# Second-layer weight sums as a stream of short steps, and another order of products in the last chunk

## The chip, the cores and the metric

The kernel runs on one core of one Trainium2 chip. Time is device time of one execution in microseconds, taken as the median of several runs of the same program. A core has five engines that run side by side, each through its own list of instructions in order: TensorE (PE; its weight loads are shown as PEld), VectorE (DVE), ScalarE (ACT), GpSimd (POOL) and SyncE (SP), which issues most DMAs here. Engines wait for one another and for DMAs by semaphores. An instruction that waits holds up all that stand behind it on its engine.

## The reference

```python
def _moe_ref(x, domain_probs, w1, w2):
    p = domain_probs / (domain_probs.sum(-1, keepdims=True) + 1e-09)
    for e in range(E):
        h = np.maximum(x @ w1[e], 0.0)
        out += p[:, e:e + 1] * (h @ w2[e])

def reference(**kwargs):
    attn_out = _attn_ref(**attn_kwargs)          # block-sparse attention
    x = attn_out.transpose(0, 2, 1, 3).reshape(B * S, H * D)
    return _moe_ref(x=x, **moe_kwargs)
```

The attention has 4 batches, 8 heads, 768 positions and 64 columns a head, with blocks of 32 positions of which each sees its neighbours, the first, the last and three sampled ones. Then 3072 tokens of 512 columns go through 4 experts of two layers, 512 to 1024 to 512, weighted by `p` and summed.

## The kernel before

**Stages.** Attention of batch 0 comes first. From then on the experts of batch b run on TensorE with the attention of batch b + 1 mixed in. The hidden columns of the four experts are cut into `NCH` = 8 chunks of 512 columns, so that a batch of experts is 8 chunks of a first layer and a second layer.

**Two-part numbers.** TensorE gets each 32-bit operand as a rounded part (a cast on ACT, L507, L543, L604, L750) and the remainder (a subtraction on POOL or DVE, L508, L544, L605, L751). Three products of parts stand for one.

**Seven products for eight.** The first layer, but for chunk 0, takes 7 products of sums of blocks where a plain 2 by 2 block product takes 8 (Strassen and Winograd). The second layer of batch 0 is plain: `second` multiplies the hidden values `hh`, `hl` by the weights `w2o` into `po`, and DVE adds the result into `oacc` (L674, L676). The second layer of batches 1 to 3 takes seven products a chunk and half (`second7`); it needs sums of blocks of `w2`.

**Where the sums are made.** During batch 0 each weight tile is split once and written back to DRAM, to be loaded ready-made for later batches: `keep1` for the first layer, `keep2` for the second (`kept2`). `split_w2` makes the plain tiles (`w2o`), and `sums_w2(c, j)` makes the sums of a pair of tiles: four subtractions `r` on DVE (L564 to L567), then for each of two tiles of 512 columns a cast `t` on ACT (L543), a subtraction on POOL (L544) and a write of 512 KB (L548). `second` calls it at two moments of every chunk, after the last product of the first and of the second tile of the half `g` = 1; after the second one the four tiles `r2` of the next chunk are loaded (L479). The tiles `t` have two buffers.

**What sets the order.** The order of the instructions on each engine is that in which the program makes them. For batch 0 the generator `experts` mixes steps of `first` and `second`: 114 steps of the first layer (p) and 192 of the second (q), by the rule at L838. Each step's follow-up work (emptying the bank, split, sums, loads) is put on the other engines' lists right there. PSUM has one bank each for `v` and `w` in batch 0; a first-layer product that starts afresh in `w` needs the last reader of that bank to be done.

**Later batches.** After the first layer of a chunk, `hidden` makes the seven operands `ho` of the second layer from the four blocks `ha` (a11, a21, a12, a22): sums on DVE or POOL, then cast and remainder. `STEPS` says how many first-layer products before or after the chunk's end each is made; at most `NHO` = 4 are ahead. `SEQ` is the order of the second layer's 14 products (number, half): numbers 1, 6, 7, 4 build up in one PSUM bank per half (`u`), the others in `v`, which has two banks. `TO` says into which of the four output blocks `tot` DVE adds each product (L812), `LAST` after which one a block is complete and goes out (L814). Weights `w2o` come through four buffers (L536). At the end of the last chunk no first layer is left to fill TensorE's waits.

Of the kernel before, what the change touches and what calls it, by code (L numbers as in the profile page):

```python
# [17 lines left out]
P = 128  # L18
# [5 lines left out]
def attention_moe_kernel(ctx: ExitStack, tc, qb, kb, vr, sampled, sampled_t, probs, w1, w2, out):  # L24
# [437 lines left out]
    ORDER2 = (1, 2, 5, 6, 3, 7, 4)  # L462
# [13 lines left out]
    def load_w2(n):  # L476
        if n < NCH * FT:
            r2[n] = raw.tile([P, DM], F32, name="r2", bufs=FT)
            nc.sync.dma_start(r2[n], w2[n // FT, n % FT])  # L479
# [47 lines left out]
    def again2():  # L527
        half = DM // 2
        for b in range(1, B):
            for c in range(NCH):  # L530
                for n in ORDER2:
# [14 lines left out]
    def keep2(c, which, s, j, o):  # L546
        kept2[c, which, s, j] = dram.tile([P, 2, DM], F32, name=f"kept2_{c}_{which}_{s}_{j}")
        nc.sync.dma_start(kept2[c, which, s, j], f32(o))  # L548

    def split_w2(n):  # L550
        if n >= NCH * FT:
            next(weights2)
            return
        c, f = divmod(n, FT)
        o = wp.tile([P, 2, DM], F32R, name="w2o")
        split(r2[n], o)
        w2t[c, f] = o
        keep2(c, 0, f // 2, f % 2, o)

    def sums_w2(c, j):  # L560
        half = DM // 2
        a, b = (r2.pop(c * FT + 2 * s + j) for s in range(2))
        b11, b12, b21, b22 = (r[:, d * half:(d + 1) * half] for r in (a, b) for d in range(2))
        nc.vector.tensor_sub(b11, b12, b11)  # L564
        nc.vector.tensor_sub(b12, b22, b12)
        nc.vector.tensor_sub(b22, b22, b11)
        nc.vector.tensor_sub(b21, b21, b22)  # L567
# [80 lines left out]
    def second(b, c, g, f, j):  # L648
# [95 lines left out]
    def hidden(b, c):  # L744

        end = b == B - 1 and c == NCH - 1

# [11 lines left out]
        yield  # L759
        a12, a22 = blk.pop((c, 0, 1)), blk.pop((c, 1, 1))  # L760
# [4 lines left out]
        two(5, a21, nc.vector if end else nc.gpsimd)  # L765
# [5 lines left out]
        two(3, a12, nc.vector if end else nc.gpsimd)  # L771
# [3 lines left out]
        two(4, a22, nc.vector if end else nc.gpsimd)  # L775
# [8 lines left out]
    LAST = {2: (0, 0), 3: (0, 1), 7: (1, 1), 4: (1, 0)}  # L784
# [3 lines left out]
    def second7(b, c, i):  # L788
        n, d = SEQ[i]
        w, h = w2o[b, c, n], ho[b, c, n]  # L790
        chain = n in (1, 6, 7, 4)
        if not chain:
            ps = later["m"].tile([P, HS], F32, name="v", bufs=2)
        elif n == 1:
            ps = W2[d] = later["m"].tile([P, HS], F32, name=f"u{d}", bufs=1)
        else:
            ps = W2[d]
        fresh = not chain or n == 1
# [6 lines left out]
        for g, dh in TO[n]:  # L805
            if c == 0 and d == 0 and n in FRESH:
                tot[g, dh] = later["a"].tile([P, 2, HS], F32, name="tot", bufs=4)
            t = tot[g, dh][:, d]
            if c == 0 and n in FRESH:
                nc.scalar.copy(t, ps)  # L810
            else:
                nc.vector.tensor_add(t, ps, t)  # L812
            if c == NCH - 1 and LAST.get(n) == (g, dh) and d:
                nc.sync.dma_start(bass.AP(out.tensor, out.offset + b * S * DM + dh * (DM // 2) * S + g * HS,  # L814
                                          [[S, P], [P * S, 2], [1, HS]]), tot.pop((g, dh)))
# [10 lines left out]
    def experts():  # L826
# [8 lines left out]
        while q < len(two):  # L835

            wait = after_first and p < len(one) and one[p][2] == 4 and q < ready(p - MORE)
            if wait or p >= min(len(one), (q * NCH * L + (OFF + MORE) * len(two)) / len(two)):  # L838
# [3 lines left out]
                if p == len(one) and q % 2:  # L842
                    convert(b + 1)
                yield T2, 2
            else:
# [4 lines left out]
                after_first = True  # L850
                if p == len(one):
                    only_raw.close()
# [30 lines left out]
        todo = [(e + at, n, i) for i, e in enumerate(ends) for at, n in STEPS]  # L883
# [43 lines left out]
    def spread_weights():  # L927
# [4 lines left out]
        later["t"] = batch0.enter_context(tc.tile_pool(name="tp", bufs=2))  # L932
        rows = later["t"].tile([P, P], F32, name="prows", bufs=1)
# [17 lines left out]
    with ExitStack() as only:  # L951
# [13 lines left out]
        for n in range(N + 3):  # L965
# [23 lines left out]
            if n == N - 7:  # L989
                for s in range(2):  # L990
                    load_w1(0, s)
                for f in range(FT):
# [117 lines left out]
```

## Time and profile before

| what | value |
|---|---|
| median of 3 runs | 1301.5 us (1298.95 to 1302.43) |
| the profiled execution | 1307.93 us |
| its span, first to last instruction | 1306.2 us |
| mean granted TensorE clock | 0.977 |
| HBM read / written | 258.00 MB / 67.68 MB |
| DMA, over the span | 249 GB/s |

An engine's share of busy time is a mean over stages with different limits, so the table of stages in the prediction is the thing to start from. A row of the timeline gives the start, the length, the engine and line, the operation with output and inputs, and in brackets the idle time of the engine before it with what ended it. "issue" there means that the profile shows nothing that was waited for.

### The profile page before, as it was taken

To read this page: it belongs to the slowest core of one execution; us is meant where nothing else is said; L and a number is where in the kernel's file an instruction comes from. 1 tells how busy PE (TensorE), PEld (TensorE's weight loads), DVE (VectorE), ACT (ScalarE), POOL (GpSimd) and SP (SyncE) were. 2 spreads that over 40 slices of the span, in tenths; PEclk is the share of its full clock that TensorE was granted. 3 is DMA by queue.
4 is the path that set the end of the run, shared out by engine and by line. 5 is a ranking of instruction groups with operands and counts; after the bars stand their busy time and mean duration, and the time that the engine had idled before them with its cause. 6 is when DMAs were issued, how large, how long until landed. Compare 5 with 4: busy or idle time off the path is not lost.

```text
span 1306.2 us, 32799 instructions
## 1 busy us (share of the span) xinstructions
PE 1233.0 (94%) x12575; PEld 1127.0 (86%) x12575; DVE 858.0 (66%) x1829; ACT 530.6 (41%) x1261; POOL 789.4 (60%) x703
## 2 busy tenths in 40 slices
PE   6778998998999899999999999999999999999997
PEld 3557777877887688999999989999999999999997
DVE  5456576666656556777766766767776776666665
ACT  4563545554554324444443324544443323222221
POOL 5443647565654346576764775767664777666663
PEclk9789899999999899999999999999999999999999
DMA  8666677888875877799886966989887778887774
GB/s 248 179 204 245 242 266 266 290 292 290 284 271 209 312 226 234 238 282 267 272 252 208 340 206 218 279 264 278 272 265 211 242 219 268 259 264 249 247 235 145
DMA packets 211176, 327.85 MB, mean 251 GB/s; under 512 B 18155, under 2 KB 118092, under 8 KB 211020
## 3 DMA queue, kind: packets, MB, share of 16 engines
q1 hardware_dynamic: 203936, 302.68, 72.1%
q0 software_dynamic: 7040, 23.07, 5.9%
q8 instruction: 100, 1.64, 0.5%
q14 instruction: 56, 0.46, 0.1%
q10 hardware_dynamic: 44, 0.00, 0.0%
HBM read 258.00 MB, written 67.68 MB: 249 GB/s over the span
## 4 chain that ended last, share of the span: by engine, by line
PE 79%; DVE 8%; issue 4%; DMA 3%; ACT 3%; POOL 2%; SPq 0%; DVEq 0%; ACTq 0%; POOLq 0%
PE w L586 19%; PE u L802 14%; PE v L586 14%; PE v L802 11%; PE po L656 6%; PE o L293 3%; PE tp L280 3%; PE s L258 2%; PE s L253 2%; PE sw L327 2%; DMA kept<-t 1%; PE ow L358 1%; DVE hl L605 1%; PE tw L348 1%; ACT hh L604 1%
## 5 line engine op out<-in xcount | busy, mean ns | idle before, releaser
L751 POOL TENSOR_TENSOR ho<-ha,ho 128x768 fp32r<-128x768 f32 x165 | 322.4, 1964 | 235.3 <-ACT ho L750 234.8
L586 PE MATMUL w<-xo,wo 128*128 128x384 f32 x1536 | 318.7, 344 | 24.9 <-DVE hl L605 19.0
L586 PEld LDWEIGHTS w<-xo,wo 128*128 128x128 f32 x1536 | 273.1, 190 | 38.3 <-DVE hl L605 22.4
L750 ACT CAST ho<-ha 128x768 fp32r<-128x768 f32 x168 | 139.3, 836 | 271.4 <-DVE ha L703 97.1
L586 PE MATMUL v<-xo,wo 128*128 128x384 f32 x1200 | 245.4, 341 | 2.3 <-DVE hl L605 2.1
L802 PE MATMUL u<-ho,w2o 128*128 128x384 f32 x1152 | 237.3, 341 | 3.7 <-issue 2.7
L586 PEld LDWEIGHTS v<-xo,wo 128*128 128x128 f32 x1200 | 214.3, 189 | 8.3 <-DVE hl L605 2.7
L802 PEld LDWEIGHTS u<-ho,w2o 128*128 128x128 f32 x1152 | 204.6, 188 | 6.5 <-issue 4.7
L802 PE MATMUL v<-ho,w2o 128*128 128x384 f32 x864 | 178.3, 342 | 0.0
L802 PEld LDWEIGHTS v<-ho,w2o 128*128 128x128 f32 x864 | 153.6, 189 | 1.3 <-DVE tot L812 0.3
L812 DVE TENSOR_TENSOR tot<-u,tot 128x384 f32<-128x384 f32 x180 | 99.3, 552 | 60.2 <-PE u L802 58.0
L656 PE MATMUL po<-w2o,hh 128*128 128x512 f32 x384 | 128.6, 417 | 6.5 <-DVE oacc L676 6.5
L812 DVE TENSOR_TENSOR tot<-v,tot 128x384 f32<-128x384 f32 x180 | 95.6, 550 | 58.3 <-PE v L802 56.0
L271 ACT ACTIVATE p<-p,mx 128x256 f32<-128x256 f32 (+1 forms) x192 | 95.4, 498 | 82.2 <-DVE mx L268 82.2
L703 DVE SCALAR_TENSOR_TENSOR ha<-ha,pb 128x384 f32<-128x384 f32 x126 | 122.7, 974 | 4.4
L138 POOL DMA_INDIRECT v<-in_vr_dram,vidx x88 | 85.6, 973 | 65.8 <-PE o L293 21.7
L508 POOL TENSOR_TENSOR wo<-r,wo 128x256 fp32r<-128x256 f32 x92 | 73.8, 808 | 71.5 <-ACT wo L507 67.0
L268 DVE CUSTOM_DVE_ANT_1 p<-s,mask 128x256 f32<-128x256 f32 (+1 forms) x192 | 69.7, 418 | 38.6 <-PE s L258 37.5
L656 PEld LDWEIGHTS po<-w2o,hh 128*128 128x128 f32 x384 | 71.3, 195 | 16.8 <-DVE oacc L676 8.1
L656 PE MATMUL po<-w2o,hl 128*128 128x512 f32 x192 | 77.7, 405 | 0.0
L293 PE MATMUL o<-v,pt 128*32 128x64 f32 x2816 | 56.6, 227 | 5.6 <-issue 3.4
L293 PEld LDWEIGHTS o<-v,pt 128*32 128x32 f32 x2816 | 47.8, 114 | 16.3 <-issue 12.1
(146 smaller groups left out, 1617.2 us busy)
## 6 DMA issues: line engine op xcount, KB each, us to landing
w2o<-kept SPq DMA_DIRECT2D x336, 256.0 KB
wo<-kept SPq DMA_DIRECT2D x318, 256.0 KB
kept<-wo SPq DMA_DIRECT2D x106, 256.0 KB
v<-in_vr_dram SPq DMA_DIRECT2D x44, 384.0 KB
kept<-w2o SPq DMA_DIRECT2D x32, 512.0 KB
kept<-t SPq DMA_DIRECT2D x32, 512.0 KB
r<-in_w_dram SPq DMA_DIRECT2D x16, 512.0 KB
r<-in_w_dram SPq DMA_DIRECT2D x32, 256.0 KB
```

Of the source, the lines that this page charges most:

```text
L138: nc.gpsimd.indirect_dma_start(out=v[:, i, 1], out_offset=None, in_=vr, element_offset=b * S * DM, in_offset=bass.IndirectOffsetOnAxis(ap= ...
L268: nc.vector.tensor_tensor_reduce(p.rearrange("p (a b) -> p a b", b=BLOCK), s[h][:n, i], mk, -SCALE, 3.0e38, ALU.add, ALU.min, mx[:n])
L271: nc.scalar.activation(p, p, AF.Exp, bias=mx[:n], scale=-1.0, accum_out=self.sums[:n, m:m + 1])
L293: nc.tensor.matmul(o[cs, m], self.pt[:, 2 * m + k, cs], vs[c][:, k, e], start=k == 0, stop=k == 1)
L508: nc.gpsimd.tensor_sub(o[:, 1], src, f32(o[:, 0]))
L586: nc.tensor.matmul(ps, w[:, wi, t], x[:, xi, t], start=fresh and m == 0, stop=m == 3 * KH - 1, skip_group_check=not fresh)
L656: nc.tensor.matmul(p, a[:, js], w[:, i], start=f == 0 and n == 0, stop=f == FT - 1 and n == 2)
L703: nc.vector.scalar_tensor_tensor(block(g, half), src, 0.0, q, op0=ALU.max, op1=ALU.mult)
L750: nc.scalar.copy(o[:, 0], src)
L751: eng.tensor_sub(o[:, 1], src, f32(o[:, 0]))
L802: nc.tensor.matmul(ps, w[:, j, wi, ds], h[:, hi, j], start=fresh and m == 0, stop=m == 5, skip_group_check=not fresh)
L812: nc.vector.tensor_add(t, ps, t)
```

## The change

`sums_w2` is now a generator, `spare`. It no longer uses the tiles `r2` that `split_w2` works on, but loads each pair of tiles of `w2` a second time (`r3`, 512 KB, one buffer, 16 loads). Each call of `next(spare)` does one short step: a load, five empty steps, two subtractions on DVE, two more, and then four times a cast and subtraction of 256 columns in one step and its write (256 KB, in pieces of 1 KB) in the next. That is 16 steps for a pair. `experts` calls it after each of its own steps once p is over 16 and makes what is left when the first layer of batch 0 ends. The tiles `t` become half as wide with four buffers. `r2` has three buffers, each loaded again at the end of `split_w2`.

In the last chunk of the last batch the second layer takes its products in the order `SEQ_END`: 1, 7, 4, 2, 5, 6, 3. Product 7 goes into a `v` bank and 4 is added onto it there; product 6 is the last in `u` and is added to three output blocks. So 20 additions to `tot` stand where 16 did. `hidden` makes the operands in the order 1, 7, 4, 2, 5, 6, 3, by `STEPS_END`, with one more sum on DVE.

```diff
-    ORDER2 = (1, 2, 5, 6, 3, 7, 4)
+    SEQ_END = [(1, 0), (7, 0), (1, 1), (7, 1), (4, 0), (4, 1), (2, 0), (2, 1),
+               (5, 0), (5, 1), (6, 0), (6, 1), (3, 0), (3, 1)]
+    def last_one(b, c):
+        return b == B - 1 and c == NCH - 1
...
-            r2[n] = raw.tile([P, DM], F32, name="r2", bufs=FT)
+            r2[n] = raw.tile([P, DM], F32, name="r2", bufs=3)
...
-        split(r2[n], o)
+        split(r2.pop(n), o)
         w2t[c, f] = o
         keep2(c, 0, f // 2, f % 2, o)
-
-    def sums_w2(c, j):
+        load_w2(n + 3)
+
+    def sums_w2():
         half = DM // 2
-        a, b = (r2.pop(c * FT + 2 * s + j) for s in range(2))
...
-        for s, r in enumerate((a, b)):
-            o = later["t"].tile([P, 2, DM], F32R, name="t2")
-            split(r, o)
-            keep2(c, 1, s, j, o)
+        for c in range(NCH):
+            for j in range(2):
+                r = raw.tile([P, 2, DM], F32, name="r3", bufs=1)
+                nc.sync.dma_start(r, w2[c, j::2].rearrange("s p e -> p s e"))
+                for _ in range(6):
+                    yield
+                b11, b12, b21, b22 = (r[:, s, d * half:(d + 1) * half] for s in range(2) for d in range(2))
+                nc.vector.tensor_sub(b11, b12, b11)
+                nc.vector.tensor_sub(b12, b22, b12)
+                yield
+                nc.vector.tensor_sub(b22, b22, b11)
+                nc.vector.tensor_sub(b21, b21, b22)
+                yield
+                for s in range(2):
+                    for d in range(2):
+                        cols = slice(d * half, (d + 1) * half)
+                        o = later["t"].tile([P, 2, half], F32R, name="t2", bufs=4)
+                        split(r[:, s, cols], o)
+                        yield
+                        keep2(c, 1, s, j, o, cols)
+                        yield
...
-            elif f < 2:
-                sums_w2(c, f)
-                if f == 1:
-                    for i in range(FT):
-                        load_w2((c + 1) * FT + i)
...
+        if last_one(b, c):
+            two(7, s3)
+            yield
+            a12, a22 = blk.pop((c, 0, 1)), blk.pop((c, 1, 1))
+            two(4, a22)
+            nc.vector.tensor_add(a21, a21, a22)
+            yield
+            two(2, a12, nc.vector)
+            nc.gpsimd.tensor_sub(a11, a21, a11)
+            yield
+            two(5, a21, nc.vector)
+            yield
+            two(6, a11)
+            nc.vector.tensor_sub(a12, a12, a11)
+            yield
+            two(3, a12, nc.vector)
...
+    STEPS_END = [(-5, 0), (-4, 1), (-3, 7), (0, 4), (0, 2), (0, 5), (0, 6), (0, 3)]
+    TO_END = {**TO, 6: [(0, 1), (1, 1), (1, 0)]}
+    LAST_END = {(0, 0): 2, (0, 1): 3, (1, 1): 6, (1, 0): 6}
...
+                if p > L + 2:
+                    next(spare, None)
```

How this stands on the engines is shown at three places. The first is DVE's list in chunk 0 of batch 0, at the first sums; `r` are raw weights and their sums, `mx` is attention's row maximum, `hl` and `p` belong to the first layer. Before:

```order
L503 TENSOR_TENSOR r_2249<-r_2249 128x256
L564 TENSOR_TENSOR r_1641<-r_1641 128x256
L565 TENSOR_TENSOR r_1641<-r_1645,r_1641 128x256
L566 TENSOR_TENSOR r_1645<-r_1645,r_1641 128x256
L567 TENSOR_TENSOR r_1645<-r_1645 128x256
L334 TENSOR_REDUCE mx_2714<-sw 128x1 x2
L336 TENSOR_TENSOR mx<-mx_2714 128x1
L337 TENSOR_SCALAR mx<-mx 128x1
L564 TENSOR_TENSOR r_1643<-r_1643 128x256
L565 TENSOR_TENSOR r_1643<-r_1647,r_1643 128x256
L566 TENSOR_TENSOR r_1647<-r_1647,r_1643 128x256
L567 TENSOR_TENSOR r_1647<-r_1647 128x256
```

The changed kernel's list, some steps further on, where its first sums stand (L578 to L582):

```order
L505 TENSOR_TENSOR r_2588<-r_2588 128x256
L578 TENSOR_TENSOR r_2761<-r_2761 128x256
L579 TENSOR_TENSOR r_2761<-r_2761 128x256
L691 TENSOR_SCALAR oacc<-po,pr 128x512
L581 TENSOR_TENSOR r_2761<-r_2761 128x256
L582 TENSOR_TENSOR r_2761<-r_2761 128x256
L659 TENSOR_TENSOR u_2846<-w,z_2814 128x384
```

Eight sums stood within twelve rows; now two and two stand between the layer's own instructions, and the second pair of tiles comes 16 steps later.

The second place is SP's list of DMAs around the same sums: `kept<-t` writes sums, `kept<-wo` first-layer weights, `r<-in_w` loads weights. Before:

```order
L548 DMA kept_0_1_0_0_2684<-t_2681 128x1024
L548 DMA kept_0_1_1_0_2689<-t_2686 128x1024
L548 DMA kept_0_1_0_1_2734<-t_2731 128x1024
L548 DMA kept_0_1_1_1_2739<-t_2736 128x1024
L479 DMA r_2741<-in_w_dram 128x512
L479 DMA r_2743<-in_w_dram 128x512
L479 DMA r_2745<-in_w_dram 128x512
L479 DMA r_2747<-in_w_dram 128x512
```

In the changed kernel, from the first load of a pair (`128x2x512`) to the next one's neighbourhood:

```order
L574 DMA r_2761<-in_w_dram 128x2x512
L492 DMA kept_1_1_2_2784<-wo 128x512
L492 DMA kept_1_1_1_2822<-wo 128x512
L492 DMA kept_1_1_5_2852<-wo 128x512
L555 DMA kept_0_1_0_0_2854<-t_2837 256x1x256
L492 DMA kept_1_1_6_2879<-wo 128x512
L555 DMA kept_0_1_0_0_2854<-t_2860 256x1x256
L132 DMA v<-in_vr_dram 96x2x512
L135 DMA v<-in_vr_dram 32x2x512
L555 DMA kept_1_0_0_0_2964<-w2o 128x1024
L485 DMA r_2966<-in_w_dram 128x512
L555 DMA kept_0_1_1_0_2974<-t_2968 256x1x256
```

The group of four writes and four loads is spread out: half writes alternate with other DMAs, and each plain tile's load follows the write of another.

The third place is DVE's list at the end of the program, from the last first-layer result (`ha<-w,pb`) on; the `u` and `v` are banks of second-layer products, `ho` an operand of them. Before:

```order
L703 SCALAR_TENSOR_TENSOR ha<-w,pb 128x384
L761 TENSOR_TENSOR ha<-ha 128x768
L751 TENSOR_TENSOR ho<-ha,ho 128x768
L812 TENSOR_TENSOR tot<-u_16989,tot 128x384
L812 TENSOR_TENSOR tot<-u_17025,tot 128x384
L812 TENSOR_TENSOR tot<-u_17252,tot 128x384
L812 TENSOR_TENSOR tot<-v,tot 128x384
L812 TENSOR_TENSOR tot<-u_17268,tot 128x384
L751 TENSOR_TENSOR ho<-ha,ho 128x768
```

Now:

```order
L720 SCALAR_TENSOR_TENSOR ha<-w,pb 128x384
L780 TENSOR_TENSOR ha<-ha 128x768
L852 TENSOR_TENSOR tot<-u_17149,tot 128x384
L852 TENSOR_TENSOR tot<-u_17185,tot 128x384
L766 TENSOR_TENSOR ho<-ha,ho 128x768
L852 TENSOR_TENSOR tot<-u_17411,tot 128x384
L852 TENSOR_TENSOR tot<-v,tot 128x384
L852 TENSOR_TENSOR tot<-u_17427,tot 128x384
L766 TENSOR_TENSOR ho<-ha,ho 128x768
```

The two additions that empty the `u` banks of the chunk before the last now stand ahead of the first subtraction for an operand. In both lists the bank names with the higher numbers belong to the last chunk.

More of the change, by code (lines that the diff above doesn't have):

```diff
@@ L530, in again2 @@
             for c in range(NCH):
-                for n in ORDER2:
+                for n in [n for n, d in (SEQ_END if last_one(b, c) else SEQ) if d]:
                     o = wp.tile([P, 2, 2, half], F32R, name="w2o")
@@ L544, in split, with keep2 @@
         nc.gpsimd.tensor_sub(o[:, 1], src, f32(o[:, 0]))
-    def keep2(c, which, s, j, o):
-        kept2[c, which, s, j] = dram.tile([P, 2, DM], F32, name=f"kept2_{c}_{which}_{s}_{j}")
-        nc.sync.dma_start(kept2[c, which, s, j], f32(o))
+    def keep2(c, which, s, j, o, cols=slice(0, DM)):
+        if (c, which, s, j) not in kept2:
+            kept2[c, which, s, j] = dram.tile([P, 2, DM], F32, name=f"kept2_{c}_{which}_{s}_{j}")
+        nc.sync.dma_start(kept2[c, which, s, j][:, :, cols], f32(o))
     def split_w2(n):
@@ L555, in split_w2 @@
         o = wp.tile([P, 2, DM], F32R, name="w2o")
-        split(r2[n], o)
+        split(r2.pop(n), o)
         w2t[c, f] = o
         keep2(c, 0, f // 2, f % 2, o)
-    def sums_w2(c, j):
+        load_w2(n + 3)
+    def sums_w2():
         half = DM // 2
-        a, b = (r2.pop(c * FT + 2 * s + j) for s in range(2))
[L563 to L567, printed above, removed]
-        for s, r in enumerate((a, b)):
-            o = later["t"].tile([P, 2, DM], F32R, name="t2")
-            split(r, o)
-            keep2(c, 1, s, j, o)
+        for c in range(NCH):
[19 more added lines that the diff above has]
+                        yield
+    spare = sums_w2()
     accs = {}
@@ L744, in hidden @@
     def hidden(b, c):
-        end = b == B - 1 and c == NCH - 1
         def two(n, src, eng=nc.gpsimd):
@@ L759, in hidden @@
         yield
+        if last_one(b, c):
[14 more added lines that the diff above has]
+            two(3, a12, nc.vector)
+            yield
+            return
         a12, a22 = blk.pop((c, 0, 1)), blk.pop((c, 1, 1))
@@ L764, in hidden @@
         yield
-        two(5, a21, nc.vector if end else nc.gpsimd)
+        two(5, a21)
         yield
@@ L770, in hidden @@
         yield
-        two(3, a12, nc.vector if end else nc.gpsimd)
+        two(3, a12)
         yield
@@ L774, in hidden @@
         yield
-        two(4, a22, nc.vector if end else nc.gpsimd)
+        two(4, a22)
         yield
@@ L783, in attention_moe_kernel @@
     FRESH = {1: (0, 0), 5: None, 4: (1, 0)}
-    LAST = {2: (0, 0), 3: (0, 1), 7: (1, 1), 4: (1, 0)}
+    LAST = {(0, 0): 2, (0, 1): 3, (1, 1): 7, (1, 0): 4}
+    TO_END = {**TO, 6: [(0, 1), (1, 1), (1, 0)]}
+    LAST_END = {(0, 0): 2, (0, 1): 3, (1, 1): 6, (1, 0): 6}
     W2 = {}
@@ L788, in second7 @@
     def second7(b, c, i):
-        n, d = SEQ[i]
+        last = last_one(b, c)
+        n, d = (SEQ_END if last else SEQ)[i]
         w, h = w2o[b, c, n], ho[b, c, n]
-        chain = n in (1, 6, 7, 4)
-        if not chain:
+        fresh = n not in ((6, 4) if last else (6, 7, 4))
+        if last and n in (7, 4):
+            if n == 7:
+                W2[7, d] = later["m"].tile([P, HS], F32, name="v", bufs=2)
+            ps = W2[7, d]
+        elif n not in (1, 6, 7, 4):
             ps = later["m"].tile([P, HS], F32, name="v", bufs=2)
-        elif n == 1:
-            ps = W2[d] = later["m"].tile([P, HS], F32, name=f"u{d}", bufs=1)
-        else:
+        else:
+            if n == 1:
+                W2[d] = later["m"].tile([P, HS], F32, name=f"u{d}", bufs=1)
             ps = W2[d]
-        fresh = not chain or n == 1
         m = 0
@@ L804, in second7 @@
             m += 1
-        for g, dh in TO[n]:
+        for g, dh in (TO_END if last else TO)[n]:
             if c == 0 and d == 0 and n in FRESH:
@@ L812, in second7 @@
                 nc.vector.tensor_add(t, ps, t)
-            if c == NCH - 1 and LAST.get(n) == (g, dh) and d:
+            if c == NCH - 1 and (LAST_END if last else LAST)[g, dh] == n and d:
                 nc.sync.dma_start(bass.AP(out.tensor, out.offset + b * S * DM + dh * (DM // 2) * S + g * HS,
@@ L850, in experts @@
                 after_first = True
+                if p > L + 2:
+                    next(spare, None)
                 if p == len(one):
+                    for _ in spare:
+                        pass
                     only_raw.close()
@@ L882, in experts @@
         made = used = 0
-        todo = [(e + at, n, i) for i, e in enumerate(ends) for at, n in STEPS]
+        todo = [(e + at, n, i) for i, e in enumerate(ends)
+                for at, n in (STEPS_END if i == len(ends) - 1 else STEPS)]
         gens = {}
@@ L931, in spread_weights @@
         nc.tensor.transpose(t[:n], pr.rearrange("p t e -> p (t e)"), ident)
-        later["t"] = batch0.enter_context(tc.tile_pool(name="tp", bufs=2))
-        rows = later["t"].tile([P, P], F32, name="prows", bufs=1)
+        later["t"] = batch0.enter_context(tc.tile_pool(name="tp", bufs=4))
+        rows = later["t"].tile([P, P], F32, name="prows", tag="t2", bufs=4)
         nc.scalar.copy(rows[:n], t[:n])
@@ L991, in attention_moe_kernel @@
                     load_w1(0, s)
-                for f in range(FT):
+                for f in range(3):
                     load_w2(f)
```

## The prediction

> **What bounds the kernel now.** I read the share of busy time first, then the program cut into its four stages, then TensorE's waits in the second stage, then the instructions around those waits. The table has the stretch, its length, busy time of PE, PEld, DVE, ACT and POOL with instruction counts, granted clock, DMA share and GB/s.
>
> ```profile
> span 1306.2 us, 32799 instructions
> PE 1233.0 (94%) x12575; PEld 1127.0 (86%) x12575; DVE 858.0 (66%) x1829; ACT 530.6 (41%) x1261; POOL 789.4 (60%) x703
> ...
> 117.00:461.00 344.00, 316.27 (x3023) 268.14 (x3024) 212.08 (x473) 167.11 (x428) 193.43 (x228) 0.96 0.77 268
> 461.00:1281.00 820.00, 814.92 (x7605) 781.34 (x7603) 568.76 (x1114) 297.22 (x638) 532.67 (x372) 1.00 0.81 250
> 1281.00:1306.30 25.30, 17.47 (x85) 16.14 (x84) 12.86 (x21) 3.67 (x5) 9.47 (x5) 0.89 0.45 151
> ```
>
> TensorE is the bound. From 461 to 1281 us (batches 1 to 3) it idles for 5 us of 820 at full clock, and the change leaves that stretch's order alone. What can be won lies in batch 0 (117 to 461), where it idles for 28 us and the clock is 0.96, and in the last 25 us. Its waits in batch 0 (sum, times, longest) are these, and they are nearly all of its idle time: 27.5 us.
>
> ```profile
> PE w L586 <- DVE hl L605: 17.7, 7, 3.5
> PE po L656 <- DVE oacc L676: 6.5, 2, 6.1
> PE w L586 <- DVE z L642: 3.3, 4, 1.5
> ```
>
> TensorE waits for DVE to empty a PSUM bank. The rows around the longest `hl` wait, in order of time, show what held DVE and ACT up (start, length, instruction, idle before it):
>
> ```profile
> 213.87 1.22 PE L586 MATMUL w<-xo,wo 128*128 128x384 f32 x6
> 214.63 0.42 DVE L564 TENSOR_TENSOR r<-r 128x256 f32<-128x256 f32 x1
> 216.25 1.29 POOL L544 TENSOR_TENSOR t<-r,t 128x512 fp32r<-128x512 f32 x1
> 216.43 1.40 DVE L567 TENSOR_TENSOR r<-r 128x256 f32<-128x256 f32 x1
> ...
> 224.88 0.62 ACT L543 CAST t<-r 128x512 fp32r<-128x512 f32 x1 [0.37 <-DVE r L567]
> 225.40 0.48 ACT L604 ACTIVATE hh<-w 128x384 fp32r<-128x384 f32 x1
> 225.92 0.56 DVE L605 SCALAR_TENSOR_TENSOR hl<-w,hh 128x384 fp32r<-128x384 f32 x1 [1.12 <-ACT hh L604]
> 226.53 2.29 PE L586 MATMUL w<-xo,wo 128*128 128x384 f32 x6 [3.47 <-DVE hl L605]
> ```
>
> The sums `r` (L564 to L567) and their casts `t` (L543) stand ahead of `hh` and `hl` on in-order engines. DVE's L567 takes 1.40 us beside POOL's L544. The six matmuls after the wait take 2.29 us where six before it took 1.22: the clock has dropped. The last chunk shows a second form, where the cast waits for a `t` buffer whose write to DRAM is under way:
>
> ```profile
> 439.67 1.27 SPq L548 DMA_DIRECT2D kept<-t  x2
> 446.77 0.62 ACT L543 CAST t<-r 128x512 fp32r<-128x512 f32 x1 [7.50 <-DMA kept<-t]
> 450.32 1.22 PE L656 MATMUL po<-w2o,hh 128*128 128x512 f32 x2 [6.08 <-DVE oacc L676]
> ```
>
> How much the cold clock adds is read from 8 us that begin at each restart; four of the six are
>
> ```profile
> 138.00:146.00 8.00, 8.00 (x30) 7.09 (x31) 4.60 (x8) 2.97 (x8) 3.23 (x5) 0.64 1.01 343
> 227.00:235.00 8.00, 8.00 (x32) 7.13 (x32) 3.57 (x7) 2.78 (x6) 2.93 (x5) 0.65 0.92 283
> 361.00:369.00 8.00, 7.54 (x147) 6.17 (x148) 4.09 (x14) 3.89 (x14) 5.35 (x8) 0.79 0.96 316
> 450.00:458.00 8.00, 7.64 (x24) 5.66 (x25) 7.06 (x8) 2.77 (x4) 4.02 (x2) 0.72 0.78 254
> ```
>
> These miss (1 − clock) × 8 = 2.9, 2.8, 1.7 and 2.2 us. The other two restarts (317 and 407) I take like the one at 361, 1.6 us each. Together 12.8 us. With the idle time, the sums cost batch 0 up to 27.5 + 12.8 = **40.3 us**, 2.5 us for each of the 16 pairs of sums.
>
> **The change part by part: batch 0.** These rows give count, then shortest, median and longest duration in ns:
>
> ```profile
> L507 ACT CAST wo<-r x87: 388/406/417, 100.2 to 423.6; 128x256 fp32r<-128x256 f32 x87
> L508 POOL TENSOR_TENSOR wo<-r,wo x87: 718/742/1444, 100.7 to 424.3; 128x256 fp32r<-128x256 f32 x87
> L543 ACT CAST t<-r x32: 614/619/624, 128.4 to 448.0; 128x512 fp32r<-128x512 f32 x32
> L544 POOL TENSOR_TENSOR t<-r,t x32: 1263/1286/1397, 129.1 to 448.7; 128x512 fp32r<-128x512 f32 x32
> L567 DVE TENSOR_TENSOR r<-r x16: 424/426/1397, 129.2 to 442.4; 128x256 f32<-128x256 f32 x16
> ```
>
> DVE's 64 sums stay, two to a step instead of four (or eight over two steps) in a row: 0.85 us ahead of an `hl` instead of 1.7. The 32 casts and subtractions of 512 columns become 64 of 256 columns. By the `wo` rows of that shape ACT does 64 × 0.406 = 26.0 us instead of 32 × 0.619 = 19.8, POOL 64 × 0.742 = 47.5 instead of 41.2. Both are spare: ACT is busy for 167 and POOL for 193 of 344 us. What counts is the longest piece in front of `hh` or `hl`: a cast of 0.41 instead of up to four of 0.62, and a POOL instruction of 0.74 beside which DVE may be held, instead of 1.29. The wait for `t` buffers goes, since each of the four half buffers is refilled a whole pair of sums, 16 steps, later. The stream has 16 × 16 = 256 steps, and the program offers 265 before the first layer of batch 0 ends, so nothing is left to be made in a lump there.
>
> What is late next: short steps beside attention's own work on DVE, and the new load `r3`. Nothing in the trace prices that directly. The bounds are nothing (the steps fit into slack) and all of today's 2.5 us a pair. I take the row nearest to it, the waits for `z`, where PE waited for one DVE instruction delayed by sums: 3.3 / 4 = 0.8 us. At one for each pair that leaves 16 × 0.8 = 13 us, without a colder clock. Gain: 40.3 − 13 = **27 us** (0 to 40).
>
> Two moved pieces I cost at nothing. `r2` has three buffers and is refilled behind each `keep2`; that load waits for the same POOL subtraction as the write in front of it on SP, and has three splits' time. The 64 smaller writes replace 32 on SP, where two of them took 1.27 us at 439.67; if SP ran late, the loads of `r1` and `r2` behind them would be late and ACT would stand.
>
> The new 16 loads of 512 KB and the writes of 1 KB pieces cost transfer time. Batch 0 keeps the DMA engines busy for 0.77 × 344 = 265 us. 8.4 MB at 268 / 0.77 = 348 GB/s adds 24 us. For the 16.8 MB of `t` I take 461 to 1281's 250 / 0.81 = 309 GB/s (its loads are mostly of short pieces), which adds 6 us. 295 us in a batch 0 of 317 us is a share of 0.93: it fits, but transfers will queue longer.
>
> **The last chunk.** In order of time:
>
> ```profile
> 1278.89 2.28 PE L802 MATMUL u<-ho,w2o 128*128 128x384 f32 x12
> 1279.56 0.95 DVE L761 TENSOR_TENSOR ha<-ha 128x768 f32<-128x768 f32 x1
> 1281.46 1.82 DVE L751 TENSOR_TENSOR ho<-ha,ho 128x768 fp32r<-128x768 f32 x1 [0.95 <-ACT ho L750]
> 1283.21 1.01 DVE L812 TENSOR_TENSOR tot<-u,tot 128x384 f32<-128x384 f32 x2
> 1283.85 2.23 PE L802 MATMUL u<-ho,w2o 128*128 128x384 f32 x6 [2.68 <-issue]
> 1287.58 1.22 PE L802 MATMUL u<-ho,w2o 128*128 128x384 f32 x6
> ...
> 1298.83 3.33 PE L802 MATMUL u<-ho,w2o 128*128 128x384 f32 x18
> ...
> 1302.21 0.56 DVE L812 TENSOR_TENSOR tot<-u,tot 128x384 f32<-128x384 f32 x1 [0.49 <-PE u L802]
> ```
>
> PE is free at 1281.2, but the next `u` bank is emptied by the adds at 1283.21, which stand behind L751 on DVE. The trace calls the wait "issue"; it ends when the first add does. In the new order the adds follow the 0.95 us sum directly: 1279.56 + 0.95 + 0.55 = 1281.1, in time. That removes 2.7 us, and the cold start behind it: two products from 1283.85 to 1287.58, 3.7 us, against 2 × 1.05 (the step from 12 to 18 matmuls, 3.33 − 2.28). That is 1.6 more. Operands 1 and 7 are both ready, so four products run (4.2 us). Then 4 accumulates on the bank of 7 and must wait for the add that reads it. Following DVE's new order with 0.55 for an add, 0.95 for a subtraction, I get waits of 0.8, 0.5 and 0.2 us at products 4, 2 and 5, against 2.0 us lost between 1287.58 and 1302.16 now: 0.5 won. At the end product 6 brings six adds (3.0 us) against 2.1 us of PE, so the last add ends some 0.8 us later behind PE than now. Sum: 2.7 + 1.6 + 0.5 − 0.8 = **4 us** (0 to 5.5).
>
> **Two rules of the Trainium skill weighed.** The clock: 1.81 us of idle stand ahead of the restart at 361, whose clock was 0.79.
>
> ```profile
> 361.46 1.60 PE L586 MATMUL w<-xo,wo 128*128 128x384 f32 x6 [1.81 <-DVE hl L605]
> ```
>
> The Trainium skill, "TensorE: Matmul & The Clock Gate", Part 1, says that the clock halves after about 3.4 us of idle window. By it only the waits of 3.47 and 6.08 us would cool (2.8 + 2.2 = 5.0 us instead of 12.8), and the gain would be 7.8 us smaller; the row of 361 speaks against it, and I keep 12.8. The second speaks against the change: "SBUF — State Buffer" says that DVE with two SBUF inputs and GpSimd exclude one another for a whole instruction. L567's 1.40 us beside L544's 1.29 agrees. By it POOL's 6.3 us more could all fall on DVE and take the gain from 31 to 25.
>
> **The rivals.** (a) *The second load is late.* DVE stands in order behind `r3`, loaded six steps earlier. Some 310 us for 265 steps make 1.2 us a step now and 1.07 after: 6.4 us. The worst transfer seen is the `kept<-t` above, 439.67 to 446.77, 7.1 us under full DMA. Late by about 2 us in half of the pairs (shorter steps, queues of 0.93 share): 8 × 2.2 = 18 us back, gain 31 − 18 = 13, time 1288. For it: the share; against: six steps are usually enough. (b) *Slower.* Same place, every pair: if TensorE loses more than (40.3 + 4) / 16 = 2.8 us a pair, the change loses. A load of 9 us holds DVE for 2.6 us, and TensorE then also restarts cold (12.8 / 6 = 2.1): 4.7 × 16 = 75, less 44, some 30 us slower: 1332; in three pairs of four 1313. It decides from about 8 us a load, above the worst seen. (c) *Not what it says:* attention's bursts, not sums, hold `hl`; then all 2.5 us a pair stay and 4 us of the tail count: 1298. Against: the waits stand only beside `r` and `t`.
>
> **How the numbers follow.** The profiled execution took 1307.9 us (span 1306.2), the median of the runs is 1301.5, 6.4 less. 1307.9 − 27 − 4 = 1276.9 there, **1270** as a median. Forecast (1256 to 1283) 0.62; (a) 0.20; (c) and mixtures within 0.3% 0.07; (b) 0.11. The range takes in no residue at all with the whole tail (40.3 + 5.5: 1256) and (a) with 4 us to spare: 1256 to 1292. 0.3% is about what a measurement of this kernel can tell from no change. Faster 0.82, same 0.07, slower 0.11.
>
> **What would show it.** Right: in 117 to 440 the waits of PE for `hl` fall from 17.7 to below 10 us, no cast waits for `kept<-t`, the clock there is near 1.00, batch 0 ends 25 us earlier, and no 2.68 us stand ahead of the last chunk. Wrong: waits of DVE's `r` for `r<-in_w`, ending in `hl`; a DMA share near 1; POOL's subtractions as the releaser of DVE.

## The result and the profile after

The changed kernel is slower: 1315.4 us median (1310.1 to 1315.7, 4 runs) against 1300.2 us (1298.0 to 1302.4, 4 runs), a ratio of 1.0107, 95% interval 1.0075 to 1.0139. The forecast was 1270 us, a gain of 31 us; the change costs 14 us by the ratio instead.

The page of the changed kernel and its stretches, taken as before: the stretch, its length, busy time of PE, PEld, DVE, ACT and POOL, granted clock, DMA share, GB/s.

```profile
span 1313.4 us, 32968 instructions
...
117.00:461.00 344.00, 306.90 (x2965) 258.33 (x2964) 206.81 (x462) 163.18 (x454) 197.28 (x256) 0.95 0.82 279
461.00:1281.00 820.00, 814.26 (x7594) 779.27 (x7593) 574.83 (x1112) 297.44 (x638) 530.92 (x372) 1.00 0.82 253
```

Batches 1 to 3 are as they were. Batch 0 got worse: TensorE idles 37 of 344 us instead of 28, at clock 0.95. From the first product of its first layer to the last `po` it takes 372.1 us (98.4 to 470.5) instead of 358.0 (103.1 to 461.1). The stretch ahead of it differs from profile to profile (96 to 105 us in the kernels below), so I compare that length, always on the profiled run.

TensorE's waits in batch 0 of the changed kernel (sum, times, longest), then DVE's in the same stretch:

```profile
PE po L678 <- DVE oacc L693: 17.7, 8, 4.5
PE w L608 <- DVE z L664: 10.4, 4, 3.8
PE po L678 <- DVE oacc L691: 5.2, 1, 5.2
PE w L608 <- DVE hl L627: 3.1, 2, 1.6
PE w L608 <- DVE u L659: 1.9, 1, 1.9
```

```profile
DVE hl L627 <- ACT hh L626: 48.6, 56, 2.8
DVE r L578 <- DMA r<-in_w_dram: 43.5, 14, 6.5
```

The wait for `hl` that the forecast wanted gone has gone, from 17.7 to 3.1 us. A new one stands in its place: DVE waits 14 times for the second load, `r<-in_w_dram` at L578, 43.5 us in all. `oacc`, `z` and `u` stand behind it on DVE and TensorE waits for those. One such place, in order of time, with the rows of SP's queue, POOL, DVE and PE that matter:

```profile
209.47 1.70 POOL L550 TENSOR_TENSOR t<-r,t 128x256 fp32r<-128x256 f32 x2
...
211.12 0.93 POOL L514 TENSOR_TENSOR wo<-s,wo 128x256 fp32r<-128x256 f32 x1
...
211.96 0.52 SPq L555 DMA_DIRECT2D kept<-t  x1
212.00 1.29 POOL L550 TENSOR_TENSOR w2o<-r,w2o 128x512 fp32r<-128x512 f32 x1
...
213.40 0.33 SPq L492 DMA_DIRECT2D kept<-wo  x1
214.39 0.52 SPq L555 DMA_DIRECT2D kept<-t  x1
215.01 0.55 SPq L555 DMA_DIRECT2D kept<-w2o  x1
215.79 0.33 SPq L485 DMA_DIRECT2D r<-in_w_dram  x1
216.44 0.68 SPq L574 DMA_DIRECT2D r<-in_w_dram  x1
...
223.00 0.42 DVE L578 TENSOR_TENSOR r<-r 128x256 f32<-128x256 f32 x1 [6.53 <-DMA r<-in_w_dram]
223.46 0.42 DVE L579 TENSOR_TENSOR r<-r 128x256 f32<-128x256 f32 x1
223.80 0.55 DVE L664 TENSOR_TENSOR z<-w,z 128x384 f32<-128x384 f32 x1
224.41 2.29 PE L608 MATMUL w<-xo,wo 128*128 128x384 f32 x6 [3.78 <-DVE z L664]
```

POOL has done its last subtraction from the one `r3` buffer at 211.2, and the refill could start. SP issues it at 216.44: it has five transfers ahead of it in its own order, four of them writes of POOL's results. POOL had finished those results 0.8 us or more before each write, so here it is not POOL that holds SP up: it begins one transfer every 0.6 to 1.4 us. DVE comes for the data 0.03 us after the issue (223.00 − 6.53 = 216.47), stands for 6.53 us, and TensorE for 3.78 us. Over all of batch 0 SP's own longest waits (same columns) are for POOL:

```profile
SPq L555 <- POOL t L550: 59.4, 29, 8.3
SPq L555 <- POOL w2o L550: 47.6, 18, 8.1
SPq L492 <- POOL wo L514: 30.8, 19, 5.3
```

Worked out in this way for the 15 loads after the first: from issue to the moment when DVE comes for it, which I call the lead in time, lie 0.03 to 7.9 us, **3.3 us on average**, where the forecast had 6.4. From the buffer's release to the issue SP takes 2.3 us on average, up to 5.3. Of these 34.9 us in all, SP spends 25.8 on issuing transfers, one to five of which stand ahead of each load, and 3.7 on waits for POOL. The 13 loads that DVE waited for took 4.3 to 7.3 us from issue to use, 6.0 on average; two of them took a little more than the forecast's bound of 7.1.

The last chunk of the changed kernel, in order of time:

```profile
1287.97 0.94 DVE L780 TENSOR_TENSOR ha<-ha 128x768 f32<-128x768 f32 x1
1288.84 1.01 DVE L852 TENSOR_TENSOR tot<-u,tot 128x384 f32<-128x384 f32 x2
1289.49 1.30 PE L842 MATMUL u<-ho,w2o 128*128 128x384 f32 x6 [0.33 <-issue]
...
1294.99 1.83 POOL L766 TENSOR_TENSOR ho<-ha,ho 128x768 fp32r<-128x768 f32 x1 [1.85 <-ACT ho L765]
1295.20 2.44 DVE L788 TENSOR_TENSOR ha<-ha 128x768 f32<-128x768 f32 x1
1295.34 1.32 PE L842 MATMUL v<-ho,w2o 128*128 128x384 f32 x6 [0.32 <-DVE tot L852]
1297.56 1.01 DVE L852 TENSOR_TENSOR tot<-v,tot 128x384 f32<-128x384 f32 x2
1298.21 6.01 PE L842 MATMUL v<-ho,w2o 128*128 128x384 f32 x24 [1.55 <-issue]
```

The 2.68 us ahead of it are 0.33 now. But a sum that I priced at 0.95 us (L788) takes 2.44 us beside a POOL subtraction of 1.83 us, and with it go 1.55 us of PE, which goes on only after the first of the two additions behind that sum.

### The profile page after: what moved, and what is told of

It is laid out like the page before. It is cut to its first block, busy times and chain, and to the rows that moved or that the text cites. A ratio compares the mean times of both kernels' runs of the same rounds, so it can differ in the third digit from the quotient of the medians.

```text
span 1313.4 us, 32968 instructions
## 1 busy us (share of the span) xinstructions
PE 1229.9 (94%) x12575; PEld 1123.8 (86%) x12575; DVE 870.8 (66%) x1834; ACT 529.4 (40%) x1293; POOL 795.1 (61%) x734
## 4 chain that ended last, share of the span: by engine, by line
PE 74%; DVE 10%; DMA 7%; issue 3%; ACT 2%; POOL 2%; SPq 1%; DVEq 0%; ACTq 0%; POOLq 0%
PE w L608 18%; PE u L842 15%; PE v L608 14%; PE v L842 11%; PE po L678 5%; DMA r<-in_w_dram 5%; PE o L293 3%; PE tp L280 3%; PE s L258 2%; DVE hl L627 2%; PE sw L327 2%; PE s L253 1%; PE ow L358 1%; ACT hh L626 1%; DMA wo<-kept 1%
## 5 line engine op out<-in xcount | busy, mean ns | idle before, releaser
L608 PEld LDWEIGHTS w<-xo,wo 128*128 128x128 f32 x1536 | 273.6, 190 | 33.2 <-DVE z L664 12.8
L842 PE MATMUL u<-ho,w2o 128*128 128x384 f32 x1128 | 231.3, 340 | 0.3 <-issue 0.3
L842 PEld LDWEIGHTS u<-ho,w2o 128*128 128x128 f32 x1128 | 199.7, 188 | 2.5 <-issue 1.2
L842 PE MATMUL v<-ho,w2o 128*128 128x384 f32 x888 | 183.6, 343 | 1.9 <-issue 1.5
L842 PEld LDWEIGHTS v<-ho,w2o 128*128 128x128 f32 x888 | 158.5, 190 | 3.5 <-issue 2.0
L678 PE MATMUL po<-w2o,hh 128*128 128x512 f32 x384 | 128.7, 417 | 23.0 <-DVE oacc L693 17.7
L720 DVE SCALAR_TENSOR_TENSOR ha<-ha,pb 128x384 f32<-128x384 f32 x126 | 126.3, 1003 | 4.3
L550 POOL TENSOR_TENSOR t<-r,t 128x256 fp32r<-128x256 f32 x64 | 52.1, 820 | 14.5 <-ACT t L549 11.9
```

The lines of the kernel that those rows point to most:

```text
L608: nc.tensor.matmul(ps, w[:, wi, t], x[:, xi, t], start=fresh and m == 0, stop=m == 3 * KH - 1, skip_group_check=not fresh)
L678: nc.tensor.matmul(p, a[:, js], w[:, i], start=f == 0 and n == 0, stop=f == FT - 1 and n == 2)
L720: nc.vector.scalar_tensor_tensor(block(g, half), src, 0.0, q, op0=ALU.max, op1=ALU.mult)
L842: nc.tensor.matmul(ps, w[:, j, wi, ds], h[:, hi, j], start=fresh and m == 0, stop=m == 5, skip_group_check=not fresh)
```

## The experiments

The theory after the first look, A: DVE waits for a load that is issued too late, since SP comes late to it, and nothing else in the stream costs much. The rival, B: the short steps or the half-wide tiles hold TensorE by themselves. Ratios are to the kernel before on the same chip, with 95% intervals; "wait" is DVE's wait for the second load; batch 0 is measured as above, on the profiled run. e2, whose instructions in batch 0 are those of before, has 361.0 us there, so a difference of 3 us between two profiles tells nothing. e13, e14 and e16 ran on a chip on which the kernel before takes 1311.5 us, and their lengths of batch 0 are to be read against that.

| run | ratio | wait, us | batch 0, us |
|---|---|---|---|
| before | 1 | none | 358.0 |
| changed kernel | 1.0107 (1.0075 to 1.0139) | 43.5 | 372.1 |
| e2 end order alone | 0.9983 (0.9967 to 0.9999) | none | 361.0 |
| e3 stream alone | 1.0113 (1.0089 to 1.0136) | 44.5 | 375.6 |
| e4 lead of 3 steps | 1.0482 (1.0453 to 1.0510) | 102.7 | 423.3 |
| e1 two `r3`, two `t` | 1.0231 (1.0207 to 1.0256) | 1.7 | 390.0 |
| e5 loads in halves, three `t` | 0.9971 (0.9954 to 0.9988) | 1.7 | 354.6 |
| e12 no second load | 0.9896 (0.9879 to 0.9913) | 2.3 | 345.1 |
| e9 refill two steps earlier | 0.9951 (0.9924 to 0.9978) | 16.2 | 351.9 |
| e8 refill on POOL's queue | 1.0043 (1.0026 to 1.0060) | 21.3 | 363.3 |
| e13 e9, low halves on DVE | 0.9993 (0.9974 to 1.0013) | 18.7 | 359.1 |
| e14 e9, every second on DVE | 1.0022 (1.0004 to 1.0040) | 24.4 | 364.7 |
| e16 changed kernel, low halves on DVE | 1.0124 (1.0085 to 1.0163) | 33.4 | 378.3 |
| e17 lead of 11, splits on end | **0.9831 (0.9814 to 0.9849)** | 4.7 | 330.8 |
| e18 e17 with a lead of 6 | 1.0094 (1.0060 to 1.0128) | 43.6 | 371.4 |
| e20 e9, begun 4 steps later | 0.9910 (0.9881 to 0.9939) | 13.5 | 345.1 |
| e19 e17 without second load | 0.9796 (0.9763 to 0.9829) | 0 | 328.7 |

### The two halves of the change apart

e2 is the kernel before with the diff's edits to the end of the last batch alone; e3 has all the others.

> The kernel before with only the new order of the last chunk. If the prediction's term for it is right, 4 us faster than before (0 to 5.5): 1294 to 1300. The 2.68 us before the last chunk's first product go; the last first-layer product to the end of the span falls from 27.2 to about 23 to 26 us. Rival: the four more additions on DVE give it all back: no change.

> The changed kernel with the last chunk's old order: only the stream of sums from the second load. If the end's order gains 1 to 4 us, this is 1 to 4 us slower than the changed kernel: 1315 to 1320 us, all of it in batch 0. If the end's order costs time: 1308 to 1314.

The end order alone gives 1298.15 us, some 2 us less; the stream alone loses what the whole change loses. From the end of the last product of the first layer to the end of the span it is 24.9 us with e2, 26.3 us in the changed kernel and 27.2 us before.

### Less lead, and a second buffer

In e1, and below, `load_pair(i)` holds the allocation and the load of the pair's `r3`; e1 has two such buffers and loads one pair ahead.

```diff
 e4
-                for _ in range(6):
+                for _ in range(3):
                     yield
 e1
-                r = raw.tile([P, 2, DM], F32, name="r3", bufs=1)
-                nc.sync.dma_start(r, w2[c, j::2].rearrange("s p e -> p s e"))
+                load_pair(2 * c + j + 1)
+                r = r3.pop(2 * c + j)
...
-                        o = later["t"].tile([P, 2, half], F32R, name="t2", bufs=4)
+                        o = later["t"].tile([P, 2, half], F32R, name="t2", bufs=2)
```

> The changed kernel with three steps between a load's issue and its first use instead of six (13 steps a pair instead of 16, so the stream ends earlier). Theory A: each pair's wait grows by up to three steps, some 3 us; DVE's waits for r<-in_w rise from 43.5 to 70 to 95 us and the time to 1330 to 1365. Theory B: the time stays within 1308 to 1325, since what counts are the steps themselves.

> The changed kernel, but with two buffers for the second load, so that each pair's load is issued one pair (16 steps, some 18 us) earlier; to make room, the half tiles t have two buffers instead of four. Theory A (the load comes too late; DVE stood 43.5 us at the first subtraction of a pair, and TensorE behind it): DVE's waits for r<-in_w fall from 43.5 to below 5 us, TensorE's idle time in batch 0 from 43 to about 20 us, and the time to 1275 to 1292 us. Theory B (short steps beside attention are what holds DVE; the wait for the load only shows where DVE stands anyway): DVE's waits go, but TensorE's idle time in batch 0 stays above 35 us, time 1305 to 1316. If the two t buffers bind, ACT waits for kept<-t instead.

Three steps less add 59 us of wait and 3.75% (49 us) to the time, 0.82 us for each us of wait. A had forecast 70 to 95 us of wait and 1330 to 1365 us; 102.7 and 1363.7 came. A later load costs more, as A says, but a pair of 13 steps also puts every step at another place. The longest wait in e4 is 14.0 us (DVE's waits in batch 0):

```profile
DVE r L578 <- DMA r<-in_w_dram: 102.7, 15, 14.0
```

Neither forecast time came with e1, and it tells nothing on B: the load's wait is gone, but the room for the second buffer came from `t`, and with two half buffers ACT waits for their writes (ACT's waits):

```profile
ACT t L549 <- DMA kept<-t: 71.7, 16, 15.3
```

It does show that the four half buffers of the changed kernel are needed.

### No second load; the load in halves, and earlier

e12 leaves out 15 of the 16 second loads and makes all sums from one tile, so batches 1 to 3 do not have the reference's values. e5 loads in halves of 256 KB into three buffers. e9 moves the refill to the place behind the fourth split, ahead of its write, two steps earlier. e8 issues it there from POOL's queue.

```diff
 e12
+                if c == j == 0:
                     r = raw.tile([P, 2, DM], F32, name="r3", bufs=1)
                     nc.sync.dma_start(r, w2[c, j::2].rearrange("s p e -> p s e"))
 e9, and e8 with nc.gpsimd.dma_start in load_pair
                         split(r[:, s, cols], o)
+                        if (s, d) == (1, 1):
+                            load_pair(2 * c + j + 1)
                         yield
                         keep2(c, 1, s, j, o, cols)
```

> Leaves out 15 of the 16 second loads: the changed kernel makes all sums again and again from the one tile that was loaded first, so the kept sums (and the batches that use them) are not those of the reference; the instructions on DVE, ACT, POOL and the kept writes are all there. Theory A (the load comes too late behind one buffer, and nothing else in the stream costs much): DVE's wait of 43.5 us for the load is gone, batch 0 ends below 345 us after its first product (372 in the changed kernel, 358 before), and the kernel takes 1265 to 1285 us. Theory B (the short steps hold TensorE by themselves, through the one tile in place, the half t buffers or SP's queue): batch 0 stays above 355 us and the kernel takes 1298 us or more.

> The second load in halves of 256 KB with three buffers: the first half of the next pair is asked for before the sums of this pair, the second half after this pair's second split; three half buffers of t in place of four, for want of room. Theory A: DVE's wait for the second load falls from 43.5 us to under 10 us and the kernel takes 1270 to 1292 us. Theory B (the stream itself holds TensorE): the wait falls as well, but the kernel stays at 1300 us or more. A third outcome, from the run with two buffers: ACT waits for the kept writes of t by more than 15 us in batch 0, and the kernel takes 1295 to 1315 us.

> One r3 buffer as in the changed kernel, but its refill stands two steps earlier in SP's order, right behind the fourth split and ahead of that split's kept write. Theory A, with the lead set by SP's order: two steps are about 2 us more lead in each of 15 pairs, so DVE's wait falls from 43.5 us to 15 to 28 us and the kernel takes 1288 to 1304 us. If the lead is set by POOL's last subtraction (the buffer) alone, the wait falls by less than 8 us and the kernel stays at 1306 to 1316 us.

> One r3 buffer, its refill issued by POOL's queue right behind the fourth split, so that it waits neither for a place in SP's order nor for another engine. Theory A: the issue comes at the moment when the buffer is free, some 2 to 4 us a pair earlier than in the changed kernel, so DVE's wait falls from 43.5 us to under 15 us; the kernel takes 1275 to 1300 us, if issuing costs POOL no more than about 1 us a load. If the transfer itself were the cause and not its start, the wait would stay above 30 us and the kernel at 1310 us or more.

Two steps in SP's order take 27 of the 43.5 us of wait away and make the kernel faster than before: the refill is now issued 0.9 us after the release on average, not 2.3, and the lead is 5.2 us, not 3.3. The load's place in SP's order set the lead. e5 has hardly any load wait, yet only 0.9971; there ACT waits 37.1 us for three `t` buffers, the third outcome. e8 still has half the wait, although POOL issues the refill 0.3 to 0.9 us after the release and the lead is 5.8 us on average: the ten loads that DVE waited for took 5.8 to 8.2 us from issue to use, 6.7 on average, and issuing takes POOL 0.75 us each.

e12 speaks against A in its plain form. Without any load it reaches 1286.8 us, just outside A's 1265 to 1285, and batch 0 is 13 us shorter than before, not 27. Half of the expected gain was missing for another reason. e9 shows what it may be: one `hl` of DVE takes 8.60 us while POOL runs subtractions on end (in order of time):

```profile
242.93 1.30 POOL L550 TENSOR_TENSOR w2o<-r,w2o 128x512 fp32r<-128x512 f32 x1
243.31 8.60 DVE L636 SCALAR_TENSOR_TENSOR hl<-z,hh 128x384 fp32r<-128x384 f32 x1 [1.19 <-ACT hh L635]
244.18 0.73 POOL L550 TENSOR_TENSOR t<-r,t 128x256 fp32r<-128x256 f32 x1
...
250.24 1.25 POOL L550 TENSOR_TENSOR w2o<-r,w2o 128x512 fp32r<-128x512 f32 x1
```

### POOL's subtractions taken away, and the steps moved

```diff
 e13 (e9's refill, one step later, behind the last of these) and e16 (the changed kernel's); e14 for d == 1 only
-                        split(r[:, s, cols], o)
+                        nc.scalar.copy(o[:, 0], r[:, s, cols])
                         yield
+                        nc.vector.tensor_sub(o[:, 1], r[:, s, cols], f32(o[:, 0]))
                         keep2(c, 1, s, j, o, cols)
 e17, from e9
-                for _ in range(6):
+                for k in range(10):
                     yield
+                    if not k and kept:
+                        keep2(*kept.pop())
...
                         split(r[:, s, cols], o)
                         if (s, d) == (1, 1):
                             load_pair(2 * c + j + 1)
-                        yield
-                        keep2(c, 1, s, j, o, cols)
+                        if kept:
+                            keep2(*kept.pop())
+                        kept.append((c, 1, s, j, o, cols))
                         yield
```

> The refill of r3 early in SP's order, as in the run that moved it two steps, and the 64 low halves of the sums made by DVE one step after ACT's cast, in place of POOL's 64 subtractions. With the refill moved and POOL left as it was, one DVE instruction hl<-z,hh that takes 0.54 us elsewhere took 8.60 us while POOL ran nine subtractions on end, others 4.02 and 2.61 us, and DVE still waited 16.2 us for the load. Theory P (POOL's run of short subtractions holds DVE and frees r3 late): no hl in batch 0 over 3 us, DVE's wait for the load under 8 us, and the kernel 1275 to 1287 us (1293.4 with the refill moved alone). Theory D (64 more instructions of about 0.42 us, 27 us, fill DVE, and TensorE waits for it instead): TensorE's waits for DVE in batch 0 above 25 us, and 1293 us or more.

> As the run with all low halves on DVE, but only every second one (32) there and 32 left on POOL. Theory P: the runs of POOL's subtractions are shorter, so the longest hl falls from 8.60 us to under 5 us, and the kernel takes 1278 to 1290 us, at or a little above the run with all on DVE. Theory D: nearer to the run with none moved (1293.4 us) and faster than the one with all on DVE.

> The changed kernel with its refill of r3 where it is, and only the 64 low halves of the sums on DVE in place of POOL. If POOL's lag is what frees the buffer late and holds SP's order, DVE's wait for the load falls from 43.5 us to 15 to 32 us and the kernel takes 1288 to 1306 us. If the place of the refill in the program alone decides, the wait stays above 36 us and the kernel at 1308 us or more.

> The refill of r3 early in SP's order as before, and the four splits of a pair in four steps on end (the kept write of each with the next split), so that ten steps lie between the refill's place in the program and the sums in place of eight. Theory A (lead alone): DVE's wait for the load falls from 16.2 us to under 6 us and the kernel takes 0.989 to 0.993 of before, from 0.995 with the refill moved alone. Theory P (POOL's subtractions, now closer together, hold DVE's instructions with two inputs in SBUF): the wait falls as well, but hl of 4 us and more stay or grow in number and the ratio is 0.994 or above.

Theory P fails as a cure: e13's longest `hl` is 1.78 us, but DVE, with 64 more instructions, makes TensorE wait 23.5 us for `z` (34 us in all), and nothing is won; e14 is no better, with a longest `hl` of 6.02 us. In e16 the wait falls to 33.4 us only, between the two outcomes named for it, and the time stays.

e17 does most of what the forecast had hoped: 1277.8 us, faster than both kernels and than either theory had said (0.989 or more). It keeps the 16 steps of a pair but puts ten between refill and sums, so that the lead in steps is 11 where e9 has 8, and the four splits on end. Its stretches of batch 0, and TensorE's and DVE's waits there:

```profile
117.00:429.00 312.00, 299.97 (x2999) 253.84 (x2998) 215.91 (x469) 164.12 (x455) 200.54 (x256) 1.00 0.90 313
```

```profile
PE po L692 <- DVE oacc L707: 7.0, 7, 1.8
PE w L622 <- DVE z L678: 2.7, 3, 1.2
PE w L622 <- DVE u L673: 1.3, 1, 1.3
PE w L622 <- DVE hl L641: 0.9, 1, 0.9
```

```profile
DVE r L588 <- DMA r<-in_w_dram: 4.7, 2, 3.7
```

The clock is 1.00 and TensorE's waits are 11.9 us, at a DMA share of 0.90. The lead is 3.3 to 11.5 us, 7.4 on average, counted as above. But e17 moves two things, the lead and the place of the steps in a chunk. e18 takes back the lead alone, e20 gives e9 the place alone, e19 leaves 15 of the 16 loads out of e17, as e12 does in the changed kernel:

```diff
 e18
                     if not k and kept:
                         keep2(*kept.pop())
+                    if k == 3 and c + j:
+                        load_pair(2 * c + j)
 e20, from e9
         load_pair(0)
+        for _ in range(4):
+            yield
```

> As the run with four splits on end, but the refill of r3 again only six steps ahead of the sums, as in the changed kernel; splits and sums stay where that run has them. Theory A (the lead decides): DVE's wait for the load, 4.7 us there, is 20 us or more, and the ratio to before is 1.000 to 1.012. Theory P (where splits and sums stand in the chunk decides, since POOL's subtractions then do not hold DVE): the ratio is 0.990 or less.

> The run that moved the refill two steps (ratio 0.9951, wait 16.2 us), with the whole stream begun four steps later, so that sums stand where the run with four splits on end has them, with the lead of eight steps unchanged. Theory P: no hl of 4 us or more is left, and the ratio is 0.985 to 0.991. Theory A: the wait stays at 12 to 20 us and the ratio at 0.992 to 0.998.

> As the run with four splits on end, leaving out 15 of the 16 second loads: all sums are made from the tile loaded first, so the later batches do not have the reference's values. Theory A, with nothing left of the load's price at ten steps of lead: within 6 us of that run (ratio 0.978 to 0.984). If the loads' traffic still cost there: a ratio under 0.976. The same cut in the stream of the changed kernel gave 0.9896; what lies between is the place of the steps in the chunk, not the load.

With every sum and split where e17 has them and the refill six steps ahead, the loss is back whole (DVE's waits of e18):

```profile
DVE r L590 <- DMA r<-in_w_dram: 43.6, 12, 8.1
```

1.0094 against 0.9831: **the lead alone is worth 2.6%, 34 us**. Without a load, the place and closeness of the steps is worth 1.0% (e12 against e19, 0.9896 and 0.9796, intervals apart), 13 us. With the load at eight steps the shift alone (e20 against e9) gives 0.4%, and the intervals overlap; e20's ratio is at the upper end of P's forecast and its wait inside A's. That POOL's hold on DVE is how the place acts fits the rows (the longest `hl` is 8.60 us in e9 and 2.25 in e17, 8.59 in e12 and 4.12 in e19) and was not isolated: e13 took it away and paid elsewhere. e19's 0.9796 beside e17's 0.9831 puts the load at some 5 us once it is early; the intervals overlap, so it may be nothing.

## Why the prediction was wrong

- **The step that failed** is in rival (a): "Some 310 us for 265 steps make 1.2 us a step now and 1.07 after: 6.4 us". Steps are the program's time, in which DVE advances. The refill's start is set by other engines: POOL's last subtraction from the one buffer, then SP, which has other transfers ahead of it in its own order. That leaves 3.3 us on average. The load's length was bounded well (7.1 against 7.3 us). e18 and e17 differ in the load's place alone. In the forecast's sum a late load had its place in the residue: 13 us for 16 pairs, 2.5 us a pair at most. Batch 0 became 14.1 us longer, so the residue was 40.3 + 14.1 = 54 us, 3.4 a pair, and half of it, 27 us, is the late load (372.1 against 345.1 in e12).
- The same step was half said where it was taken as free: "if SP ran late, the loads of `r1` and `r2` behind them would be late and ACT would stand". SP did run late; what stood was DVE, since `r3` is the one load without a second buffer.
- Rival (b) had the place and nearly the price: 2.6 us a load were worked out, 43.5 / 16 = 2.7 came, and its 1313 to 1332 us hold the 1315.4. That the time fits is partly luck: (b) set 56 to 75 us of loss against 44 of gain, while the load cost 27 us and the stream without it gained 14 (e12). Its chance of 0.11 was too small because its condition, loads of 8 us or more, was the wrong one: a 6 us load is enough when the lead is 3 us.
- **The ceiling was nearly right, for another order of steps.** In e17 batch 0 is 358.0 − 330.8 = 27.2 us shorter on the profiled runs, the 27 of the sum; TensorE's waits fall from 27.5 to 11.9 us (the residue taken was 13) and the clock is 1.00. The waits are 15.6 of the 27.2 us; the other 11.6 go with the clock (0.96 before), close to the 12.8 us that the sum had for it. Between medians e17 gains 22 us of the 31 forecast, 2 of them by the end order, so some 20 in batch 0: that the two profiled runs give just 27 is in part luck.
- **The other half of the residue** is not the load. In the changed kernel's own order, even without the loads (e12), batch 0 is 13 us shorter and not 27, which leaves 40.3 − 13 = 27 us, 1.7 a pair. 0.8 is only reached in e17's and e19's order of steps; why the order matters stays open. "A POOL instruction of 0.74 beside which DVE may be held" was too small: DVE can be held for a whole run of them (8.60 us in e9, 7.37 us in the changed kernel).
- "The wait for `t` buffers goes" was right with four half buffers, and e1 and e5 show that it comes back with two or three. The DMA share, forecast 0.93, is 0.90 in e17: the traffic fits.
- The last chunk: the 2.68 us went, as worked out. The 4 us missed that the subtraction of L788 would take 2.44 us (2.43 in e2), not 0.95; e2 measures a gain of 2 us.
- The forecast's signs of "wrong" named the row that came, DVE's `r` for `r<-in_w`; it ended in `oacc` and `z` rather than `hl`.

## What to carry to other kernels

Count the lead of a load from the moment when its buffer is free and its queue has come to it, not from its place in the program: on an in-order queue the transfers ahead of it, writes that wait for their producers among them, set the start. With one buffer, put the refill right behind the last reader and ahead of that reader's write, and give it more steps than the transfer needs. When a stream of small steps is fitted between other work, try where in the period its steps fall before changing what they do.

## What the runs showed of the hardware

DVE instructions with two inputs in SBUF were held through a run of POOL instructions, not one. In batch 0 of e9, `hl` by its first input (count, then shortest, median and longest in ns); `w` and `v` lie in PSUM, `p`, `u` and `z` in SBUF:

```profile
L636 DVE SCALAR_TENSOR_TENSOR hl<-w,hh x16: 544/558/559, 119.1 to 437.6; 128x384 fp32r<-128x384 f32 x16
L636 DVE SCALAR_TENSOR_TENSOR hl<-p,hh x14: 558/559/4020, 133.8 to 426.7; 128x384 fp32r<-128x384 f32 x14
L636 DVE SCALAR_TENSOR_TENSOR hl<-u,hh x14: 557/559/660, 143.4 to 433.3; 128x384 fp32r<-128x384 f32 x14
L636 DVE SCALAR_TENSOR_TENSOR hl<-z,hh x14: 557/707/8598, 149.9 to 435.7; 128x384 fp32r<-128x384 f32 x14
L636 DVE SCALAR_TENSOR_TENSOR hl<-v,hh x2: 558/558/558, 116.8 to 122.4; 128x384 fp32r<-128x384 f32 x2
```

Those with an input in PSUM never took over 0.56 us; one with both in SBUF took 8.60 us, during which POOL began nine subtractions without a gap. The Trainium skill, "SBUF — State Buffer", section "SBUF: two separate sides", has the lock of the shared ports for one whole instruction; the rows agree, and show in addition that DVE did not get in between POOL's instructions while they followed on end.
